# Three batches of q and k turned on TensorE from 128 partitions, and loads and weights in order of need

## The chip, the cores and the metric

The kernel runs on one core of a Trainium2 chip. The metric is the device time of one execution in microseconds (us); "the span" is the time from the first to the last instruction in a profiled execution, some 2 us less. Most fast executions of a kernel here agree within 1 to 1.5%. Each has a state, fast or slow, from its time against the fastest run of the same kernel; comparisons below use fast runs. A profile belongs to one execution.

Engines: PE is TensorE, DVE is VectorE, ACT is ScalarE, POOL is GpSimd, and SP is the engine whose queue issues nearly all DMAs here. "SPq" and "POOLq" are the queues. An "evacuation" is the copy of a matmul's or transpose's result out of PSUM, the memory that PE writes.

## The reference, cut to what matters

B = 8 batches, H = 8 heads, S = 576 tokens, 16 beacon keys and values ahead of them, D = 64. Then an FFN with three input weights and a maximum.

```python
scores = scale * q @ concat(beacon_k, k).T        # causal on the 576 tokens, beacons always seen
a = softmax(scores);  x = a @ concat(beacon_v, v) # x: 4608 tokens x 512
h = maximum(maximum(x @ w1, x @ w2), x @ w3)      # 512 -> 768
out = h @ w_out                                   # 768 -> 512, float32
```

## The kernel before

A "pair" is two heads of one batch; there are 32 pairs, numbered 0 to 31, four to a batch. Each pair needs q and k with D on the partitions, so q and k must be turned. Batches 0 and 1 are turned on PE; batches 2 to 7 are cast to bfloat16, stored to DRAM and fetched back by a transposing DMA into `qT` and `kT`. Attention of a pair and a share of the FFN alternate, so that PE has work while ACT computes exponentials.

Loads go through nine rotating staging buffers (`st`) and a list. Every cast of a staged item by `C(...)` issues the next load of the list:

```python
st_pool = tc.tile_pool(name="st", bufs=9)

def load_pair(p, k_queue=None):                     # 96 partitions, two runs of 1536 bytes in each
    ...
    queue.dma_start(
        out=st[0:QP, i * NQ2 : (i + 1) * NQ2].rearrange("p (h x) -> p h x", h=2),
        in_=src[b, hs].rearrange("h (p r) d -> p h (r d)", r=QR))      # QR = 6, QP = 96

loads = [L(load_pair, p, nc.scalar) for p in range(PPB)]
loads += [L(load_v, 0, 0), L(load_v, 0, 1)]
for b in range(1, B):
    loads += [L(load_pair, b * PPB + i) for i in range(PPB)]
    if b == 1:
        loads += [L(load_beacons, B_PE, B, bk32)]
    loads += [L(load_v, b, 0), L(load_v, b, 1)]

def C(fn, *a):
    def run():
        fn(*a)
        next_load()          # one load for one cast
    return run

def start():
    load_beacons(0, B_PE, bk32_0)
    next_load(10)
    ...                      # cast pair 0
    next_load()

# p is the first pair of batch b >= 2; plan entries are (pair, step)
at_step(p - 3, 0, L(open_dram, b))
at_step(p + 1, 0, C(cast_v, b, 0, by_pool))         # v is cast one pair after its batch has begun
at_step(p + 1, 1, C(cast_v, b, 1, by_pool))
for i in range(PPB):
    at_step(p + i - 4 + (p + i == 8), 0, C(cast_pair, p + i, by_pool, by_pool))
    at_step(p + i - 3, int(p + i == 8), L(store_pair, p + i))
    at_step(p + i - 2, 1, L(fetch_pair, p + i))
```

Loads, stores to DRAM, fetches and output stores stand in the one SP queue, in program order; only k of batch 0 goes by ACT's queue and the weights by POOL's. The masks of pairs 4 and later and all casts but pair 0's are POOL's.

The softmax here doesn't subtract the row's maximum and nothing guards it: scores larger than these inputs give would overflow.

Of the kernel before, what the change touches and what calls it, by code (L numbers as in the profile page):

```python
# [9 lines left out]
BF16 = mybir.dt.bfloat16  # L10
# [6 lines left out]
def kernel(  # L17
# [27 lines left out]

    QR = 6
    QP = S // QR
    HALF = S // 2
# [14 lines left out]
    B_PE = 2  # L63
# [88 lines left out]
    def load_pair(p, k_queue=None):  # L152
        b, g, j0 = place(p)
        hs = slice(head(g, j0), head(g, j0) + 2)
        st = new_stage(("pair", p))
        for i, (src, queue) in enumerate(((q, nc.sync), (k, k_queue or nc.sync))):
            queue.dma_start(  # L157
                out=st[0:QP, i * NQ2 : (i + 1) * NQ2].rearrange("p (h x) -> p h x", h=2),
                in_=src[b, hs].rearrange("h (p r) d -> p h (r d)", r=QR),
            )  # L160

    def cast_piece(p, i, cast, r0=0, r1=QR):
        st = stage["pair", p]
        if ("pair16", p, i) not in stage:
            stage["pair16", p, i] = pair_pool.tile([QP, QR, 2, D], BF16, name=f"p16{i}")
        cast(  # L166
            stage["pair16", p, i][:, r0:r1].rearrange("p r h d -> p h r d"),
            st[0:QP, i * NQ2 : (i + 1) * NQ2].rearrange(
                "p (h r d) -> p h r d", h=2, r=QR
            )[:, :, r0:r1],  # L170
        )
# [63 lines left out]
    def turn_beacons():  # L235
        ps = ffn_psum.tile([128, PPB, NB_PE], BF16, name="fps")
        for pi in range(PPB):
            nc.tensor.transpose(
                ps[:, pi],
                bk16_0[:, 2 * pi : 2 * pi + 2].rearrange("p h d -> p (h d)"),  # L240
                ident[0:NB_PE, 0:NB_PE],
            )
        by_act(bT, ps)
# [31 lines left out]
    def turn(p, i, ps):  # L275
        src = stage.pop(("pair16", p, i))
        for r in range(QR):
            nc.tensor.transpose(
                ps[:, r * QP : (r + 1) * QP],
                src[:, r].rearrange("p h d -> p (h d)"),  # L280
                ident[0:QP, 0:QP],
            )

    def evac_q(p, ps, copy):
        copy(
            qTs[p % NT].rearrange("d (p r) -> d p r", r=QR),
            ps.rearrange("d (r p) -> d p r", r=QR),
        )

    def evac_k(p, ps, copy):  # L290
        b, pi = divmod(p, PPB)
        kT = kTs[p % NT]
        copy(kT[:, 0:Nb], bT[:, pi, Nb * b : Nb * (b + 1)])
        copy(
            kT[:, Nb:NK].rearrange("d (p r) -> d p r", r=QR),
            ps.rearrange("d (r p) -> d p r", r=QR),
        )

    def turn_pair(p, apart, q_copy=None, k_copy=None):
# [3 lines left out]
        else:  # L303
            both = sc_psum.tile([128, 2, 1024], BF16, name="sc")
# [184 lines left out]
    for tb in range(n_tokb):  # L489
        last_b = (TOKB * (tb + 1) - 1) // S  # L490
        for ft in range(n_ft):
            for i in range(3):
                units.append((last_b, mm1_unit, (tb, ft, i)))
# [23 lines left out]
    loads = [L(load_pair, p, nc.scalar) for p in range(PPB)]  # L517
    loads += [L(load_v, 0, 0), L(load_v, 0, 1)]
    for b in range(1, B):
        loads += [L(load_pair, b * PPB + i) for i in range(PPB)]  # L520
        if b == 1:
            loads += [L(load_beacons, B_PE, B, bk32)]
        loads += [L(load_v, b, 0), L(load_v, b, 1)]
# [13 lines left out]
    def start():  # L537
        load_beacons(0, B_PE, bk32_0)
        keep_busy(12)
        next_load(10)  # L540
        by_pool(bk16_0, bk32_0)
        turn_beacons()
        cast_piece(0, 0, by_dve)
        cast_piece(0, 1, by_act, 0, 3)
        cast_piece(0, 1, by_dve, 3, QR)
        stage.pop(("pair", 0))
        next_load()
        turn_pair(0, True, q_copy=by_act)
# [15 lines left out]
    at_step(0, 3, L(load_w, 0, 0, FH))  # L564
    at_step(1, 0, C(cast_v, 0, 0, by_pool))
    at_step(1, 1, L(load_w, 1, 0, FH))
    at_step(1, 2, C(cast_v, 0, 1, by_pool))
    at_step(1, 3, L(load_w, 2, 0, FH))
    at_step(2, 2, C(cast_pair, 4, by_pool, by_pool))
    at_step(3, 0, L(load_w, 0, FH, d_ff))  # L570
    at_step(3, 1, L(load_w, 1, FH, d_ff))
    at_step(3, 2, C(cast_pair, 5, by_pool, by_pool))
    at_step(3, 3, L(load_w, 2, FH, d_ff))
    at_step(4, 0, L(load_w_out))
    at_step(4, 1, C(cast_pair, 6, by_pool, by_pool))
    at_step(4, 3, C(cast_v, 1, 0, by_pool))
    at_step(5, 0, C(cast_v, 1, 1, by_pool))
    at_step(5, 0, C(cast_pair, 7, by_pool, by_pool))
    at_pv(2, 0, 0, 0, 0, 1)
# [10 lines left out]
    at_step(4, 2, L(by_pool, bk16, bk32))  # L590
    for b in range(B_PE, B):
        p = b * PPB
        at_step(p - 3, 0, L(open_dram, b))
        at_step(p + 1, 0, C(cast_v, b, 0, by_pool))
        at_step(p + 1, 1, C(cast_v, b, 1, by_pool))
        for i in range(PPB):
            at_step(p + i - 4 + (p + i == 8), 0, C(cast_pair, p + i, by_pool, by_pool))
            at_step(p + i - 3, int(p + i == 8), L(store_pair, p + i))
            at_step(p + i - 2, 1, L(fetch_pair, p + i))

    def emit_all():
# [3 lines left out]
        for p in range(NPAIR):  # L605
# [3 lines left out]
            for s, gs in enumerate(steps(p)):  # L609
# [12 lines left out]
                else:  # L622
                    n_step += 1
                    allowed = (n_step - 1) * UPB / (2 * PPB) - 1
                emit_ffn(allowed)
                store_y(n_y)
# [6 lines left out]
                if not fine and nxt < B_PE * PPB and s == 0:  # L633
                    turn_pair(nxt, False, None, by_act)
# [50 lines left out]
```

## Time and profile before

340.59 us median of 3 runs (340.47 to 341.17). The profiled span was 338.9 us.

| stretch (bounds are the first scores of pairs 5 and 12) | us |
|---|---|
| start to pair 5 | 38.2 |
| pair 5 to pair 12 (seven pairs) | 79.8 |
| pair 12 to the end | 220.9 |

The windows view of the kernel before, one line for each stretch. Columns: the stretch and its length, busy time of PE, PE's weight loads, DVE, ACT and POOL with the number of instructions, the granted clock of TensorE, the mean busy share of the DMA engines, and GB/s.

```profile
0.00:38.20 38.20, 28.93 (x409) 15.59 (x410) 20.09 (x53) 21.13 (x31) 24.81 (x42) 1.00 1.12 222
38.20:118.00 79.80, 51.48 (x608) 25.11 (x616) 29.45 (x57) 29.77 (x46) 32.29 (x61) 0.85 1.04 219
118.00:338.90 220.90, 209.21 (x2329) 107.42 (x2352) 120.70 (x219) 89.46 (x136) 73.76 (x147) 0.98 0.60 137
```

In the middle stretch PE is busy 51.5 of 79.8 us, at a mean clock of 0.85, while the DMA engines are full at 219 GB/s. The waits view of PE in the same kernel names what it waits for (total us, times, longest):

```profile
PE sc L345 <- DMA kT<-k_dram: 17.3, 6, 9.5
PE pv L407 <- POOL at_sb L370: 12.5, 2, 6.3
```

The timeline of PE places them (start, duration, work, and in brackets the idle time before and what ended it): two waits for masks near 44 and 51 us, one for `kT` of pair 8 near 74 us.

```profile
50.51 0.42 PE L407 MATMUL pv<-at_sb,ones 128*32 128x288 bf16 x4 [6.21 <-POOL at_sb L370]
57.24 0.58 PE L407 MATMUL pv<-at_sb,ones 128*32 128x176 bf16 x6 [6.31 <-POOL at_sb L370]
...
83.94 0.90 PE L345 MATMUL sc<-qT,kT 64*128 64x288 bf16 x8 [9.49 <-DMA kT<-k_dram]
```

The first masks are late because POOL's queue stood at the cast of v of batch 1, which had not landed. The timeline of POOL from 48.66 us on:

```profile
48.66 1.46 POOL L210 CAST v_sb<-st 128x1536 bf16<-128x1536 f32 x1 [9.05 <-DMA st<-in_v_dram]
...
52.15 4.68 POOL L166 CAST p<-st 96x768 bf16<-96x768 f32 x6
56.78 1.73 POOL L370 TENSOR_SCALAR_AFFINE_SELECT at_sb<-at_sb 128x256 bf16<-128x256 bf16 x5
```

```profile
143.38 0.54 PE L345 MATMUL sc<-qT,kT 64*128 64x288 bf16 x8 [2.03 <-DMA kT<-k_dram]
...
175.92 0.56 PE L345 MATMUL sc<-qT,kT 64*128 64x288 bf16 x8 [2.04 <-DMA kT<-k_dram]
...
209.96 0.54 PE L345 MATMUL sc<-qT,kT 64*128 64x288 bf16 x8 [1.94 <-DMA kT<-k_dram]
```

### The profile page before, as it was taken

What the parts mean: (1) busy time and instruction counts of PE and PEld (TensorE: products, weight loads), DVE (VectorE), ACT (ScalarE), POOL (GpSimd) and SP (SyncE); (2) the same over time, 40 slices, a digit from 0 to 9 for tenths busy, and PEclk for the clock granted to TensorE, in tenths of its full rate; (3) what the DMA queues carried; (4) which work ended last, traced back from release to release, by engine and by line L of the source; (5) the groups of instructions that cost most, each with busy time, mean ns of one, the idle gap of its engine ahead of it and who ended that gap; (6) DMA issues with size and microseconds to landing.
All of it is one profiled execution on the core that took longest, in us unless ns stands there. A gap on an engine that the chain in (4) does not pass through costs nothing.

```text
span 338.9 us, 8218 instructions
## 1 busy us (share of the span) xinstructions
PE 289.6 (85%) x3342; PEld 148.1 (44%) x3372; DVE 170.2 (50%) x328; ACT 140.4 (41%) x212; POOL 130.9 (39%) x249
## 2 busy tenths in 40 slices
PE   4798622870998999799979997999999999999995
PEld 2345301330443454354435455774445445444442
DVE  0686400650546454545554555455675666555453
ACT  2468730340444564365434643454554642020220
POOL 1795529212364346345623562356523320000000
PEclk9999975995899999999998999899999999999999
DMA  8999999999959996999899979945740400301203
GB/s 198 218 248 240 196 219 242 214 241 228 227 149 239 222 242 182 230 227 200 243 222 207 162 235 217 169 112 161 141 72 35 130 0 4 124 0 49 78 0 124
DMA packets 97814, 56.32 MB, mean 166 GB/s; under 512 B 72432, under 2 KB 93168, under 8 KB 97776
## 3 DMA queue, kind: packets, MB, share of 16 engines
q1 hardware_dynamic: 92896, 51.47, 68.3%
q0 software_dynamic: 4048, 3.15, 6.0%
q10 hardware_dynamic: 832, 1.18, 1.4%
q8 instruction: 26, 0.43, 0.5%
q14 instruction: 12, 0.10, 0.1%
HBM read 35.13 MB, written 16.61 MB: 153 GB/s over the span
## 4 chain that ended last, share of the span: by engine, by line
PE 68%; DMA 8%; SPq 3%; issue 2%; DVE 1%; POOL 1%; DVEq 0%
PE fps L453 33%; PE fps L470 11%; PE pv L407 10%; PE sc L345 7%; DMA kT<-k_dram 5%; PE sc L453 5%; DMA st<-in_q_dram 2%; PE sc L470 2%; SPq L194 1%; SPq L270 1%; SPq L263 1%; SPq L157 1%; POOL at_sb L370 0%; DVE hT L463 0%; DVE xT L430 0%
## 5 line engine op out<-in xcount | busy, mean ns | idle before, releaser
L354 ACT ACTIVATE at_sb<-sc 128x992 bf16<-128x992 f32 (+3 forms) x128 | 103.9, 861 | 115.7 <-PE sc L345 115.5
L453 PE MATMUL fps<-xT,w_sb 128*128 128x512 bf16 (+1 forms) x623 | 137.5, 357 | 1.7 <-issue 0.7
L463 DVE TENSOR_TENSOR hT<-hT,fps 128x512 bf16<-128x512 bf16 x95 | 65.2, 686 | 74.4 <-PE fps L453 72.2
L453 PEld LDWEIGHTS <-w_sb 128*128 128x128 bf16 x720 | 67.1, 98 | 73.0 <-issue 14.3
L370 POOL TENSOR_SCALAR_AFFINE_SELECT at_sb<-at_sb 128x256 bf16<-128x256 bf16 (+2 forms) x140 | 51.0, 384 | 116.8 <-ACT at_sb L354 116.8
L345 PE MATMUL sc<-qT,kT 64*128 64x288 bf16 (+4 forms) x384 | 38.5, 297 | 21.2 <-DMA kT<-k_dram 17.3
L166 POOL CAST p<-st 96x768 bf16<-96x768 f32 x62 | 49.3, 824 | 18.2 <-DMA q_dram<-p 9.8
L461 DVE CAST hT<-fps 128x512 bf16<-128x512 f32 x42 | 28.9, 687 | 27.3 <-PE fps L453 27.3
L470 PE MATMUL fps<-w_out_sb,hT 128*128 128x512 bf16 x173 | 41.7, 380 | 0.8 <-DVE hT L463 0.4
L478 DVE COPY y<-fps 128x512 f32<-128x512 f32 x30 | 20.7, 689 | 30.3 <-PE fps L470 30.3
L345 PEld LDWEIGHTS <-kT 64*128 64x128 bf16 x384 | 14.0, 96 | 48.9 <-issue 25.2
L407 PE MATMUL pv<-at_sb,v_sb 128*32 128x96 bf16 (+8 forms) x1408 | 32.3, 243 | 0.0
L407 PE MATMUL pv<-at_sb,ones 128*32 128x288 bf16 (+4 forms) x512 | 19.6, 272 | 14.4 <-POOL at_sb L370 12.5
L430 DVE TENSOR_TENSOR xT<-pv,recip 128x288 bf16<-128x288 f32 (+2 forms) x96 | 28.1, 348 | 6.4 <-ACT recip L427 3.8
L470 PEld LDWEIGHTS <-hT 128*128 128x128 bf16 x216 | 20.0, 98 | 25.8 <-issue 2.0
L407 PEld LDWEIGHTS <-v_sb 128*32 128x32 bf16 (+1 forms) x1408 | 26.6, 103 | 2.8 <-issue 0.8
L210 POOL CAST v_sb<-st 128x1536 bf16<-128x1536 f32 (+2 forms) x24 | 21.0, 894 | 9.4 <-DMA st<-in_v_dram 9.4
L425 ACT ACTIVATE lnd<-pv 128x288 f32<-128x288 f32 x32 | 13.2, 412 | 24.0 <-PE pv L407 23.3
L407 PEld LDWEIGHTS <-ones 128*32 128x32 bf16 (+1 forms) x512 | 11.4, 100 | 22.3 <-issue 17.8
L453 PE MATMUL sc<-xT,w_sb 128*128 128x512 bf16 x74 | 19.2, 379 | 0.1
L427 ACT ACTIVATE recip<-lnd 128x288 f32<-128x288 f32 x32 | 14.2, 443 | 1.0
L461 ACT CAST hT<-fps 128x512 bf16<-128x512 f32 x6 | 3.5, 586 | 22.7 <-PE fps L453 22.7
(38 smaller groups left out, 90.1 us busy)
## 6 DMA issues: line engine op xcount, KB each, us to landing
st<-in_q_dram SPq DMA_DIRECT2D x32, 288.0 KB, 4.4
out_dram<-y SPq DMA_DIRECT2D x36, 256.0 KB, 2.3
st<-in_k_dram SPq DMA_DIRECT2D x28, 288.0 KB, 4.7
st<-in_v_dram SPq DMA_DIRECT2D x24, 256.0 KB, 5.5
q_dram<-p SPq DMA_DIRECT2D x24, 144.0 KB, 2.7
k_dram<-p SPq DMA_DIRECT2D x24, 144.0 KB, 2.8
w_sb<-in_moe_w_dram POOLq DMA_DIRECT2D x12, 192.0 KB, 11.3
st<-in_v_dram SPq DMA_DIRECT2D x8, 224.0 KB, 5.6
```

Source lines behind the costliest of these rows:

```text
L166: cast(stage["pair16", p, i][:, r0:r1].rearrange("p r h d -> p h r d"), st[0:QP, i * NQ2 : (i + 1) * NQ2].rearrange("p (h r d) -> p h r d" ...
L210: cast(v_sb[0:n, t:t1].rearrange("p t h d -> p (t h d)"), st[0:n, (t - t_lo) * H * D : (t1 - t_lo) * H * D],)
L345: nc.tensor.matmul(ps[:, e, off : off + q1 - q0], kT[hs, 128 * t : 128 * t + 128], qT[hs, q0:q1], start=True, stop=True, tile_position=(64 ...
L354: nc.scalar.activation(out=both_heads(p, gi), in_=ps[:, :, 0 : g_width[gi]], func=AF.Exp, scale=scale)
L370: nc.gpsimd.affine_select(out=view, in_=view, compare_op=ALU.is_ge, fill=0.0, base=x0, pattern=[[0, 2], [1, hi - lo]], channel_multiplier=-1,)
L407: nc.tensor.matmul(ps[32 * j : 32 * j + 32, bank, lo + q0 - qa : lo + qb - qa], lhsT, at_view(PPQ * quad + j // 2, t, j % 2, q0, qb), star ...
L430: nc.vector.tensor_mul(xT[:, 2 * g + part - 1, c0 + ca : c0 + cb], ps[:, bank, lo : lo + cb - ca], recip[:, ca:cb],)
L453: nc.tensor.matmul(ps[:, o0 : o0 + n], w_in[i][:, ct, 128 * ft : 128 * (ft + 1)], xT[:, ct, x0 : x0 + n], start=(ct == 0), stop=(ct == n_c ...
L461: (by_act if alone[0] else by_dve)(hT[:, ft, :], ps)
L463: nc.vector.tensor_max(hT[:, ft, :], hT[:, ft, :], ps)
L470: nc.tensor.matmul(ps, hT[:, ft, 128 * tt : 128 * (tt + 1)], w_out_sb[:, ft, :], start=(ft == 0), stop=(ft == n_ft - 1),)
L478: nc.vector.tensor_copy(y, ps)
```

## The change

Intent: (1) q and k of batches 0 to 2 land on all 128 partitions (each head on 64, nine rows of 256 bytes in a run) and are turned by 64 by 64 transposes, two side by side; so batch 2 no longer goes through DRAM, and its pairs are cast two pairs ahead of their use, not four. (2) The FFN takes one weight after the other within a block, so that w2, w3 and w_out may come later, and the weights are loaded whole, half of them behind v of batch 1. (3) Pair 0's loads come first; the second group of beacon loads comes later; the FFN's pace is a little faster at the start.

```diff
-    B_PE = 2
+    B_PE = 3
@@ load_pair
+            if b < B_PE:
+                queue.dma_start(
+                    out=st[:, i * PR * D : (i + 1) * PR * D],                       # PR = 9
+                    in_=src[b, hs].rearrange("h (p r) d -> (h p) (r d)", r=PR))
@@ turn
-        for r in range(QR):
-            nc.tensor.transpose(ps[:, r * QP : (r + 1) * QP], src[:, r]..., ident[0:QP, 0:QP])
+        for r in range(PR):
+            for e in range(2):
+                hs = slice(64 * e, 64 * e + 64)
+                nc.tensor.transpose(ps[hs, r * PP : (r + 1) * PP], src[hs, r],
+                                    ident[hs, hs], tile_position=(64 * e, 64 * e))
@@ FFN units
-        for ft in range(n_ft):
-            for i in range(3):
+        for i in range(3):
+            for ft in range(n_ft):
@@ list of loads
+    loads = [L(load_pair, 0, nc.scalar), L(load_beacons, 0, B_PE, bk32_0)]
+    loads += [L(load_pair, 1, nc.scalar)] + load_pairs(2, 4) + load_v_pieces(0)
+    loads += load_pairs(4, 8) + load_v_pieces(1)
+    loads += load_pairs(8, 12) + load_v_pieces(2) + [L(load_beacons, B_PE, B, bk32)]
+    for b in range(B_PE, B): ...
@@ start
-        load_beacons(0, B_PE, bk32_0)
         next_load(10)
@@ weights
-    (w1, w2, w3 in halves at pairs 0, 1 and 3, w_out at pair 4)
+    at_step(1, 1, L(load_w, 0, 0, d_ff))
+    at_step(3, 1, L(load_w, 1, 0, d_ff))
+    at_step(4, 2, L(load_w, 2, 0, d_ff))
+    at_step(5, 1, L(load_w_out))
@@ casts of batch 2
+    for p in range(8, B_PE * PPB):
+        at_step(p - 2, 1, C(cast_pair, p, by_pool, by_pool))
@@ emit_all
-                    allowed = (n_step - 1) * UPB / (2 * PPB) - 1
+                    allowed = n_step * UPB / 9 if n_step <= 9 else (n_step - 1) * UPB / (2 * PPB)
@@ (cut: the turn moves from the first to the second step of a pair and into another PSUM pool;
@@  evacuations, the other casts and the order of the start follow; k of pairs 2 and 3 now comes by SP)
```

More of the change, by code (lines that the diff above doesn't have):

```diff
@@ L47 @@
     QP = S // QR
+    PR = 9
+    PP = S // PR
     HALF = S // 2
@@ L156, in load_pair, with cast_piece @@
         for i, (src, queue) in enumerate(((q, nc.sync), (k, k_queue or nc.sync))):
-            queue.dma_start(
-                out=st[0:QP, i * NQ2 : (i + 1) * NQ2].rearrange("p (h x) -> p h x", h=2),
-                in_=src[b, hs].rearrange("h (p r) d -> p h (r d)", r=QR),
-            )
-    def cast_piece(p, i, cast, r0=0, r1=QR):
-        st = stage["pair", p]
-        if ("pair16", p, i) not in stage:
-            stage["pair16", p, i] = pair_pool.tile([QP, QR, 2, D], BF16, name=f"p16{i}")
-        cast(
-            stage["pair16", p, i][:, r0:r1].rearrange("p r h d -> p h r d"),
-            st[0:QP, i * NQ2 : (i + 1) * NQ2].rearrange(
-                "p (h r d) -> p h r d", h=2, r=QR
-            )[:, :, r0:r1],
-        )
+            if b < B_PE:
+                queue.dma_start(
+                    out=st[:, i * PR * D : (i + 1) * PR * D],
+                    in_=src[b, hs].rearrange("h (p r) d -> (h p) (r d)", r=PR),
+                )
+            else:
+                queue.dma_start(
+                    out=st[0:QP, i * NQ2 : (i + 1) * NQ2].rearrange("p (h x) -> p h x", h=2),
+                    in_=src[b, hs].rearrange("h (p r) d -> p h (r d)", r=QR),
+                )
+    def cast_piece(p, i, cast):
+        st = stage["pair", p]
+        if p < B_PE * PPB:
+            t16 = pair_pool.tile([128, PR, D], BF16, name=f"t16{i}")
+            cast(
+                t16.rearrange("x r d -> x (r d)"), st[:, i * PR * D : (i + 1) * PR * D]
+            )
+        else:
+            t16 = pair_pool.tile([QP, QR, 2, D], BF16, name=f"p16{i}")
+            cast(
+                t16.rearrange("p r h d -> p h r d"),
+                st[0:QP, i * NQ2 : (i + 1) * NQ2].rearrange("p (h r d) -> p h r d", h=2, r=QR),
+            )
+        stage["pair16", p, i] = t16
     def cast_pair(p, q_cast, k_cast):
@@ L235, in turn_beacons @@
     def turn_beacons():
-        ps = ffn_psum.tile([128, PPB, NB_PE], BF16, name="fps")
+        ps = pv_psum.tile([128, PPB, NB_PE], BF16, name="pv")
         for pi in range(PPB):
@@ L276, in turn @@
         src = stage.pop(("pair16", p, i))
-        for r in range(QR):
-            nc.tensor.transpose(
-                ps[:, r * QP : (r + 1) * QP],
-                src[:, r].rearrange("p h d -> p (h d)"),
-                ident[0:QP, 0:QP],
-            )
+        for r in range(PR):
+            for e in range(2):
+                hs = slice(64 * e, 64 * e + 64)
+                nc.tensor.transpose(
+                    ps[hs, r * PP : (r + 1) * PP],
+                    src[hs, r],
+                    ident[hs, hs],
+                    tile_position=(64 * e, 64 * e),
+                )
     def evac_q(p, ps, copy):
         copy(
-            qTs[p % NT].rearrange("d (p r) -> d p r", r=QR),
-            ps.rearrange("d (r p) -> d p r", r=QR),
+            qTs[p % NT].rearrange("d (p r) -> d p r", r=PR),
+            ps.rearrange("d (r p) -> d p r", r=PR),
         )
@@ L294, in evac_k @@
         copy(
-            kT[:, Nb:NK].rearrange("d (p r) -> d p r", r=QR),
-            ps.rearrange("d (r p) -> d p r", r=QR),
+            kT[:, Nb:NK].rearrange("d (p r) -> d p r", r=PR),
+            ps.rearrange("d (r p) -> d p r", r=PR),
         )
@@ L303, in turn_pair @@
         else:
-            both = sc_psum.tile([128, 2, 1024], BF16, name="sc")
+            both = pv_psum.tile([128, 2, 1024], BF16, name="pv")
             q_ps, k_ps = both[:, 0, 0:S], both[:, 1, 0:S]
@@ L515, in L, with load_v_pieces, load_pairs @@
         return lambda: fn(*a)
-    loads = [L(load_pair, p, nc.scalar) for p in range(PPB)]
-    loads += [L(load_v, 0, 0), L(load_v, 0, 1)]
-    for b in range(1, B):
-        loads += [L(load_pair, b * PPB + i) for i in range(PPB)]
-        if b == 1:
-            loads += [L(load_beacons, B_PE, B, bk32)]
-        loads += [L(load_v, b, 0), L(load_v, b, 1)]
+    def load_v_pieces(b):
+        return [L(load_v, b, 0), L(load_v, b, 1)]
+    def load_pairs(p0, p1):
+        return [L(load_pair, p) for p in range(p0, p1)]
+    loads = [L(load_pair, 0, nc.scalar), L(load_beacons, 0, B_PE, bk32_0)]
+    loads += [L(load_pair, 1, nc.scalar)] + load_pairs(2, 4) + load_v_pieces(0)
+    loads += load_pairs(4, 8) + load_v_pieces(1)
+    loads += load_pairs(8, 12) + load_v_pieces(2) + [L(load_beacons, B_PE, B, bk32)]
+    for b in range(B_PE, B):
+        loads += load_pairs(b * PPB, (b + 1) * PPB) + load_v_pieces(b)
     def next_load(n=1):
@@ L537, in start @@
     def start():
-        load_beacons(0, B_PE, bk32_0)
-        keep_busy(12)
+        keep_busy(14)
         next_load(10)
+        cast_piece(0, 0, by_dve)
+        cast_piece(0, 1, by_act)
+        stage.pop(("pair", 0))
         by_pool(bk16_0, bk32_0)
-        turn_beacons()
-        cast_piece(0, 0, by_dve)
-        cast_piece(0, 1, by_act, 0, 3)
-        cast_piece(0, 1, by_dve, 3, QR)
-        stage.pop(("pair", 0))
-        next_load()
-        turn_pair(0, True, q_copy=by_act)
+        next_load()
+        q_ps = ffn_psum.tile([128, S], BF16, name="fps")
+        k_ps = ffn_psum.tile([128, S], BF16, name="fps")
+        turn(0, 0, q_ps)
+        turn(0, 1, k_ps)
+        evac_q(0, q_ps, by_act)
+        turn_beacons()
+        evac_k(0, k_ps, by_dve)
         C(cast_pair, 1, by_pool, by_pool)()
@@ L563 @@
     at_step(0, 2, C(cast_pair, 3, by_pool, by_pool))
-    at_step(0, 3, L(load_w, 0, 0, FH))
     at_step(1, 0, C(cast_v, 0, 0, by_pool))
-    at_step(1, 1, L(load_w, 1, 0, FH))
+    at_step(1, 1, L(load_w, 0, 0, d_ff))
     at_step(1, 2, C(cast_v, 0, 1, by_pool))
-    at_step(1, 3, L(load_w, 2, 0, FH))
-    at_step(2, 2, C(cast_pair, 4, by_pool, by_pool))
-    at_step(3, 0, L(load_w, 0, FH, d_ff))
-    at_step(3, 1, L(load_w, 1, FH, d_ff))
-    at_step(3, 2, C(cast_pair, 5, by_pool, by_pool))
-    at_step(3, 3, L(load_w, 2, FH, d_ff))
-    at_step(4, 0, L(load_w_out))
-    at_step(4, 1, C(cast_pair, 6, by_pool, by_pool))
-    at_step(4, 3, C(cast_v, 1, 0, by_pool))
+    at_step(1, 3, C(cast_pair, 4, by_pool, by_pool))
+    at_step(2, 3, C(cast_pair, 5, by_pool, by_pool))
+    at_step(3, 1, L(load_w, 1, 0, d_ff))
+    at_step(4, 0, C(cast_pair, 6, by_pool, by_pool))
+    at_step(4, 1, C(cast_v, 1, 0, by_pool))
+    at_step(4, 2, L(load_w, 2, 0, d_ff))
     at_step(5, 0, C(cast_v, 1, 1, by_pool))
     at_step(5, 0, C(cast_pair, 7, by_pool, by_pool))
+    at_step(5, 1, L(load_w_out))
+    for p in range(8, B_PE * PPB):
+        at_step(p - 2, 1, C(cast_pair, p, by_pool, by_pool))
+    for b in range(2, B):
+        p = b * PPB
+        at_step(p + 1, 0, C(cast_v, b, 0, by_pool))
+        at_step(p + 1, 1, C(cast_v, b, 1, by_pool))
     at_pv(2, 0, 0, 0, 0, 1)
@@ L589 @@
         at_pv(2 * quad + 3, 0, quad, 1)
-    at_step(4, 2, L(by_pool, bk16, bk32))
+    at_step(7, 1, L(by_pool, bk16, bk32))
     for b in range(B_PE, B):
@@ L593 @@
         at_step(p - 3, 0, L(open_dram, b))
-        at_step(p + 1, 0, C(cast_v, b, 0, by_pool))
-        at_step(p + 1, 1, C(cast_v, b, 1, by_pool))
         for i in range(PPB):
-            at_step(p + i - 4 + (p + i == 8), 0, C(cast_pair, p + i, by_pool, by_pool))
-            at_step(p + i - 3, int(p + i == 8), L(store_pair, p + i))
+            at_step(p + i - 4, 0, C(cast_pair, p + i, by_pool, by_pool))
+            at_step(p + i - 3, 0, L(store_pair, p + i))
             at_step(p + i - 2, 1, L(fetch_pair, p + i))
@@ L623, in emit_all @@
                     n_step += 1
-                    allowed = (n_step - 1) * UPB / (2 * PPB) - 1
+                    allowed = n_step * UPB / 9 if n_step <= 9 else (n_step - 1) * UPB / (2 * PPB)
                 emit_ffn(allowed)
+                if not fine and nxt < B_PE * PPB and s == 1:
+                    turn_pair(nxt, False)
                 store_y(n_y)
@@ L632, in emit_all @@
                 finish_pv()
-                if not fine and nxt < B_PE * PPB and s == 0:
-                    turn_pair(nxt, False, None, by_act)
                 while emit_ffn(allowed):
```

## The prediction

> **What bounds the kernel now.** The windows view splits the 338.9 us into three regimes. From 118 us on TensorE is nearly always busy (most 20 us windows: 18 to 19.9 us); the change alters little there. From 0 to 38 us pairs 0 to 4 run at about 5 us each, set by the exponentials and the chain between PE, ACT and DVE. From 38 to 93 us TensorE starves at a DMA share near 1.1: the waits view gives PE 12.5 us on the masks (near 44 and 51 us) and 9.5 us on kT of pair 8 (at 74 us), at a granted clock of 0.5 to 0.87. The timeline shows why. First, GpSimd sits 9.05 us for v of batch 1 (cast at 48.7 us), because four weights (3.15 MB) and six beacon loads shared the engines ahead of it. Second, pair 8's store leaves the SP queue only at 75.7 us, behind saturated loads, and then needs a transposing fetch.
>
> **Removed.** Ahead of v of batch 1, the data fall from about 10.5 MB (the slices' GB/s summed to 48.6 us) to about 8.7 MB; at the measured 220 GB/s that is 8 to 9 us, so v lands near 40 us and the first stall shrinks from 12.5 to about 3 us. Batch 2 loses its DRAM round trip: 16 transfers of 144 KB, 2.3 MB, about 10 us of DMA, with the 9.5 us wait and kT waits of 1.6 and 0.2 us near 110 and 118 us. Pair 0 comes first: the first scores (11.4 us) gain 2 us.
>
> **Added.** A pair's turn goes from 12 transposes (0.68 us warm, 1.14 cold) to 36. The Trainium skill's "TensorEngine Tiling (Array Packing)", section Instruction Overhead, gives about 60 cycles per matmul, hence my estimate of 0.9 to 1.2 us warm, 1.5 to 2 us cold: about 8 us over twelve pairs, 3 of them hidden. DVE gets 8 more evacuations of 0.75 us, off the path. FFN weight by weight only lets w2, w3 and w_out come late.
>
> **On the path.** PE's work between pair 5's and pair 12's first scores: seven pairs of attention (2.5 us each), six turns (1.1), 35 FFN units (148 matmuls at 0.228 us): 58 us, against 79.8 us now (38.2 to 118.0). With 3 us for v and 2 to 4 us where GpSimd meets pair 12's load too early (14.7 MB must have moved, 66 us), pair 12 starts at 102 to 105 us instead of 118. That is 15 us, of which 0 to 2 are given back later through longer kT waits. Tail unchanged.
>
> **Predicted:** 325 us, 8 in 10 between 315 and 334. Faster by over 2%: 0.86; within 2%: 0.11; slower: 0.03.
>
> **What shows it.** The timeline: pair 12's first scores near 103 us; v of batch 1 cast near 40 us; no DMA wait at pair 8; PE waits on masks under 5 us; 36 transposes in 0.9 to 1.2 us; from pair 12 to the end still 220 to 223 us.
>
> **What would make it wrong.** GpSimd's in-order queue: a cast waiting for a late load (v of batch 1 now stands before pair 4's last masks; pair 12's cast) blocks masks, so stalls move instead of vanish. Late w3 or w_out would stall the FFN. The DMA, still behind at pair 12, could make kT waits recur. The 64 by 64 transposes may not overlap in pairs, and cost 2 us or more warm.

## The result, and the profile after

308.34 us median of 4 runs (306.05 to 309.71), against 340.88 us (340.47 to 345.34) for the kernel before over the runs by then. The ratio is 0.9012, 95% interval 0.8919 to 0.9105: faster. A ratio is the mean time of one kernel's fast runs over that of the other's of the same rounds, so it is not quite the ratio of the medians. The profile is of the fastest run, with a span of 304.3 us. The measured time lies below the predicted range of 315 to 334 us.

The windows view of the kernel after, cut at the first scores of pairs 5 and 12 as before:

```profile
0.00:37.00 37.00, 29.44 (x556) 16.52 (x556) 20.08 (x52) 21.44 (x31) 17.62 (x34) 1.00 1.04 260
37.00:93.20 56.20, 51.42 (x798) 26.03 (x812) 36.99 (x73) 28.28 (x42) 30.77 (x63) 1.00 1.03 242
93.20:304.30 211.10, 204.52 (x2325) 105.14 (x2348) 120.24 (x218) 89.45 (x136) 73.89 (x148) 1.00 0.64 146
```

| stretch | before, us | after, us | predicted, us |
|---|---|---|---|
| start to pair 5 | 38.2 | 37.0 | about 38 |
| pair 5 to pair 12 | 79.8 | 56.2 | 64 to 67 (pair 12 at 102 to 105) |
| pair 12 to the end | 220.9 | 211.1 | 220 to 223 |

So 23.6 us were gained where the prediction expected about 15, and 9.8 us where it expected nothing. In the middle stretch PE is busy as long as before (51.4 us), but of 28.3 us of idle time 4.8 are left, and the clock stays at 1.00. The waits of PE on masks and on `kT` by DMA are gone from the profile; in their place stand small waits on DVE's evacuation of the turn:

```profile
PE sc L361 <- DVE kT L310: 5.6, 6, 2.8
PE pv L423 <- DVE xT L446: 1.5, 3, 0.6
```

The timeline of PE shows a turn of 36 transposes in 0.76 us, and pair 15, which waited 2.03 us before, starting without a gap:

```profile
41.50 0.76 PE L293 MATMUL pv<-ident,t 64*64 64x64 bf16 x36
...
113.69 2.84 PE L469 MATMUL fps<-xT,w_sb 128*128 128x512 bf16 x12
116.47 0.54 PE L361 MATMUL sc<-qT,kT 64*128 64x288 bf16 x8
```

And POOL casts v of batch 1 with no wait, at 34.7 and 39.9 us (48.66 and 51.04 before), in the timeline of POOL:

```profile
34.74 1.46 POOL L223 CAST v_sb<-st 128x1536 bf16<-128x1536 f32 x1
...
39.86 1.16 POOL L223 CAST v_sb<-st 128x512 bf16<-128x512 f32 x2
```

Of the 9.8 us after pair 12, the three `kT` waits at pairs 15, 19 and 23 in the kernel before (its timeline of PE is above) are 6.0 us (2.03 + 2.04 + 1.94). Another 3.2 us are a low clock: from pair 19 to 20 and from 23 to 24 the kernel before took 8.7 us, where it took 7.1 from pair 15 to 16 with the same work. In the windows view of the kernel before, around pair 19, the clock falls after the gap:

```profile
171.00:173.00 2.00, 2.00 (x11) 0.90 (x10) 1.55 (x5) 1.56 (x2) 0.77 (x2) 1.00 1.02 195
173.00:175.00 2.00, 0.88 (x4) 0.19 (x2) 1.36 (x2) 0.00 (x0) 0.04 (x1) 1.00 1.11 149
175.00:177.00 2.00, 1.08 (x20) 0.74 (x24) 0.00 (x0) 0.59 (x1) 0.00 (x0) 0.83 0.87 292
177.00:179.00 2.00, 2.00 (x60) 1.67 (x56) 0.00 (x0) 1.08 (x2) 1.53 (x4) 0.50 1.00 247
```

The question is then what removed these waits, since nothing in the change is addressed to pairs 15, 19 and 23, and what fed the middle stretch faster than foreseen.

### The profile page after: what moved, and what is told of

It is laid out like the page before. It is cut to its first block, busy times and chain, and to the rows that moved or that the text cites. A ratio compares the mean times of both kernels' runs of the same rounds, so it can differ in the third digit from the quotient of the medians.

```text
span 304.3 us, 8877 instructions
## 1 busy us (share of the span) xinstructions
PE 285.4 (94%) x3673; PEld 147.7 (49%) x3710; DVE 177.3 (58%) x343; ACT 139.2 (46%) x208; POOL 122.3 (40%) x243
## 4 chain that ended last, share of the span: by engine, by line
PE 86%; DVE 6%; issue 2%; ACT 2%; DMA 1%; SPq 0%; POOL 0%; POOLq 0%; DVEq 0%
PE fps L469 41%; PE pv L423 12%; PE fps L486 12%; PE sc L361 10%; PE sc L469 5%; PE sc L486 2%; DVE qT L301 1%; DVE kT L310 1%; DMA bk<-in_beacon_k_dram 1%; PE fps L330 1%; DVE xT L446 1%; DVE hT L479 1%; ACT at_sb L370 1%; DVE kT L309 1%; PE fps L293 1%
## 5 line engine op out<-in xcount | busy, mean ns | idle before, releaser
L469 PEld LDWEIGHTS <-w_sb 128*128 128x128 bf16 x720 | 65.7, 97 | 71.0 <-issue 13.4
L386 POOL TENSOR_SCALAR_AFFINE_SELECT at_sb<-at_sb 128x256 bf16<-128x256 bf16 (+2 forms) x140 | 51.1, 384 | 114.5 <-ACT at_sb L370 114.5
L361 PE MATMUL sc<-qT,kT 64*128 64x288 bf16 (+4 forms) x384 | 37.7, 294 | 6.3 <-DVE kT L310 5.6
L486 PE MATMUL fps<-w_out_sb,hT 128*128 128x512 bf16 x172 | 40.6, 379 | 1.0 <-issue 0.8
L180 POOL CAST p<-st 96x768 bf16<-96x768 f32 x40 | 31.8, 822 | 0.0
L423 PE MATMUL pv<-at_sb,v_sb 128*32 128x96 bf16 (+8 forms) x1408 | 29.4, 230 | 0.0
L423 PEld LDWEIGHTS <-v_sb 128*32 128x32 bf16 (+1 forms) x1408 | 24.4, 97 | 2.2 <-issue 0.9
L423 PE MATMUL pv<-at_sb,ones 128*32 128x288 bf16 (+4 forms) x512 | 17.5, 258 | 1.6 <-DVE xT L446 1.5
L469 PE MATMUL sc<-xT,w_sb 128*128 128x512 bf16 x71 | 18.3, 380 | 0.1
L479 DVE TENSOR_TENSOR hT<-hT,sc 128x512 bf16<-128x512 bf16 x12 | 8.2, 687 | 12.5 <-PE sc L469 6.8
```

The costliest lines, as they stand in the source:

```text
L180: cast(t16.rearrange("p r h d -> p h r d"), st[0:QP, i * NQ2 : (i + 1) * NQ2].rearrange("p (h r d) -> p h r d", h=2, r=QR),)
L361: nc.tensor.matmul(ps[:, e, off : off + q1 - q0], kT[hs, 128 * t : 128 * t + 128], qT[hs, q0:q1], start=True, stop=True, tile_position=(64 ...
L386: nc.gpsimd.affine_select(out=view, in_=view, compare_op=ALU.is_ge, fill=0.0, base=x0, pattern=[[0, 2], [1, hi - lo]], channel_multiplier=-1,)
L423: nc.tensor.matmul(ps[32 * j : 32 * j + 32, bank, lo + q0 - qa : lo + qb - qa], lhsT, at_view(PPQ * quad + j // 2, t, j % 2, q0, qb), star ...
L469: nc.tensor.matmul(ps[:, o0 : o0 + n], w_in[i][:, ct, 128 * ft : 128 * (ft + 1)], xT[:, ct, x0 : x0 + n], start=(ct == 0), stop=(ct == n_c ...
L479: nc.vector.tensor_max(hT[:, ft, :], hT[:, ft, :], ps)
```

## The experiments

Eighteen kernels ran, all with correct results. "Pair 12 at" is the start of its first scores in the profile of that kernel. Kernels of one call share the runs of the kernel before, whose median was 340 to 344 us in each call; so a difference between calls is better read from the ratios, which use fast runs alone. The medians count all runs: without its one slow run, a_lead has 322.6, b_wide 332.5 and less_again 306.4 us. The profile of b_wide is of its slow run.

| kernel | edit, on the kernel before (b) or after (a) | median, us | ratio to before | pair 12 at |
|---|---|---|---|---|
| before | | 340.6 | 1 | 118.0 |
| after | | 308.3 | 0.901 | 93.2 |
| b_lead, b_less | nine, eight loads at the start, not ten | 327.4, 323.1 | 0.959, 0.947 | 113.1, 110.2 |
| a_lead | one load more ahead | 323.2 | 0.943 | 95.5 |
| b_wide | wide loads, batches 0 and 1 | 333.6 | 0.974 | 114.5 |
| b_order | weights and FFN in order of need | 340.4 | 0.997 | 119.4 |
| b_wol, b_wol_less | all three; nine, eight loads | 323.1, 320.1 | 0.945, 0.931 | 110.3, 107.0 |
| a_desc | wide loads in runs of 768 bytes | 313.1 | 0.916 | 99.3 |
| a_ft | FFN units in the old order | 314.8 | 0.922 | 102.5 |
| a_wearly | weights early and in halves | 314.7 | 0.918 | 101.8 |
| a_pace | the old pace of the FFN | 309.7 | 0.908 | 95.8 |
| after_again | none | 307.9 | 0.903 | 95.5 |
| a_lead_less, less_again | eight loads at the start | 305.7, 306.8 | 0.893, 0.899 | 92.3, (disturbed) |
| best3, best_lead, best_bpe4 | attempts at a faster kernel | 309.9, 305.7, 311.0 | 0.907, 0.893, 0.907 | 95.6, 92.5, 93.4 |
| a_probe | five layouts of loads behind the end | | | |

### The lead of the loads

The lead is how many loads have been issued ahead of the casts that use them. Each cast issues one load. The list of the kernel after has two beacon items, that of the kernel before had one, and a beacon item uses up a cast's turn without using a staging buffer. From there on every load of the kernel after is issued one cast later than before. Why that can matter: a load needs the buffer of the item nine places earlier in the list, but v of a batch is cast later than its place in the list (at the second pair of its batch, when the first pair of the next batch is already cast). With the longer lead the newest load must wait for that cast; it waits at the head of SP's queue, and the stores and fetches behind it wait too. The Trainium skill says in "DMA: Bandwidth & Descriptors", section "Anatomy of one DMA — SWDGE (gpsimd) path", that a semaphore wait of a DMA is done on the issuing sequencer before dispatch. The timeline of SP in the kernel before agrees: after the fetch at 124.23 us the queue issues nothing for 3.7 us, then the load that had waited for v's buffer and all that had gathered behind it, and the fetch for pair 15, due at 141.4, leaves at 138.8 and 140.7 us.

```profile
124.23 1.27 SPq L271 DMA_TRANSPOSE kT<-k_dram  x1
129.24 0.31 SPq L157 DMA_DIRECT2D st<-in_q_dram  x1
...
138.77 1.86 SPq L270 DMA_TRANSPOSE qT<-q_dram  x1
140.67 1.26 SPq L271 DMA_TRANSPOSE kT<-k_dram  x1
```

In the waits view of SP, the loads' wait for v's buffer is, in the kernel before from pair 12 to pair 31 and in the kernel after over the whole span:

```profile
SPq L157 <- POOL v_sb L210: 11.0, 3, 3.7
SPq L166 <- POOL v_sb L223: 1.6, 1, 1.6
```

In the kernel after, the same fetch leaves at 110.0 and 111.2 us, for a pair that starts at 116.5. The rival was that there is simply less DMA traffic, since batch 2 no longer goes through DRAM.

**a_lead** gives the kernel after the old lead back.

```diff
-    loads += load_pairs(8, 12) + load_v_pieces(2) + [L(load_beacons, B_PE, B, bk32)]
+    loads += load_pairs(8, 12) + load_v_pieces(2)
+    at_step(4, 1, L(load_beacons, B_PE, B, bk32))
```

> The kernel after, but the second beacon load is issued on its own instead of taking one turn in the list of loads, so every later load is issued one cast earlier (the lead the kernel before had). Theory (SP's in-order queue is held by a load that waits for a staging buffer, and the fetches behind it come late): SP waits on the casts of v return (16 us in total before, 1.6 us after), PE waits about 2 us for kT at pairs 15, 19 and 23 again, and the time rises by 5 to 9 us over 308. Rival (the waits vanished because there is less DMA traffic): no kT waits, within 2 us of 308.

323.22 us median (321.77 to 326.86, one of them slow), 15 us over the kernel after, more than expected. In the waits view of PE stands:

```profile
PE sc L361 <- DMA kT<-k_dram: 12.7, 4, 3.9
```

The waits view of SP in the same kernel, from 93 us to 256 us, has the wait for v's buffers again:

```profile
SPq L166 <- POOL v_sb L223: 12.3, 3, 4.1
```

The waits stand at pairs 12, 15, 19 and 23 (2.64, 3.12, 3.93, 2.97 us), and the clock is 0.50 to 0.60 after the first three and 1.00 after the fourth. From pair 12 to pair 31 it took 160.6 us, against 145.2 in the kernel after and 154.5 in the kernel before. Why these waits are longer than the three of 2 us in the kernel before was not traced.

**b_lead** takes one item of lead from the kernel before, **b_less** two; nothing else.

```diff
-        next_load(10)
+        next_load(9)       # b_lead;  next_load(8) in b_less
```

> The kernel before, with nine loads issued at the start instead of ten, so every load comes one cast later; nothing else. Theory (lead): the three 2 us kT waits at pairs 15, 19 and 23 shrink or vanish, with the low clock that follows two of them, and the time falls by 5 to 9 us from 341 to about 333. Rival (DMA traffic of batch 2's round trip): the waits stay, 339 to 342.

> The kernel before with eight loads at the start instead of ten (b_lead had nine: 327.4 us). If the order in SP's queue still costs there, the kT wait of pair 8 (9.5 us before, 7.3 us with nine) falls to 3 to 6 us and the time to 321 to 326. If pair 8 waits for bytes, not for order: 326 to 330.

b_lead: 327.43 us median (326.44 to 328.88), 13 us or more gained by one number, where 5 to 9 were expected. From pair 12 to pair 31 it took 145.2 us, exactly as in the kernel after, though batch 2 still went through DRAM: the lead alone accounts for the whole gain between those pairs, and the rival falls. Pair 12 itself comes 4.9 us earlier. SP's waits view from 113 to 258 us:

```profile
SPq L157 <- POOL v_sb L210: 3.3, 3, 1.7
```

b_less: 323.07 us (320.38 to 325.11). Its wait for pair 8 fell to 3.4 us as expected, and it has the mask waits that the kernel before had, as the waits view of PE in b_less shows:

```profile
PE pv L407 <- POOL at_sb L370: 12.4, 2, 6.3
PE sc L345 <- DMA kT<-k_dram: 3.7, 2, 3.4
```

Pair 8 starts at 77.9 us, 6 us earlier than before. So a part of the early stall at pair 8 was the place of its store and fetch behind loads that were not needed yet. b_order and b_wol below show what is left.

### The rate of the loads

**b_wide** puts only the wide layout (and its transposes) for batches 0 and 1 into the kernel before. The diff is the `load_pair` and `turn` parts shown above with `B_PE = 2`.

> The kernel before, with only the layout of q and k of batches 0 and 1 changed to 128 partitions and 36 small transposes; batch 2 still goes through DRAM, weights and order as before. Theory (DMA rate): v of batch 1 is cast about 5 to 6 us earlier than 48.7 us, the two mask waits (12.5 us) shrink to about 7, kT of pair 8 is still waited for, and the time falls by 4 to 9 us from 341. Rival (only the order of the weights matters): 339 to 344.

333.59 us median of 4, one of them slow; the fast ones 331.27 to 334.67, ratio 0.974 (0.964 to 0.985), which does not settle "over 2%" by its interval. The profile fell in the slow run. A gain of about 9 us is at the upper end of what was expected, although the transposes tripled in number. In that profile v of batch 1 was cast at 44.4 us, 4.3 us earlier and not 5 to 6, and the mask waits were 10.7 us, not about 7: 6.3 of them are still the casts of pairs 7 to 9.

**a_desc** keeps the 128 partitions but lands each run of 2304 bytes as three of 768.

```diff
-                    out=st[:, i * PR * D : (i + 1) * PR * D],
-                    in_=src[b, hs].rearrange("h (p r) d -> (h p) (r d)", r=PR),
+                    out=gapped(st, i),        # three pieces of 192 floats in each 256
+                    in_=src[b, hs].rearrange("h (p c r) d -> (h p) c (r d)", c=3, r=3),
```

> The kernel after, with each partition's 2304 contiguous bytes of a pair load of batches 0 to 2 landed as three runs of 768 bytes with gaps, same partitions, same bytes, same order. Theory (longer runs move faster: 350 to 390 GB/s against 250 to 275): the GB/s while pairs load fall to 250 or lower, v of batch 1 lands later by 5 us or more, PE waits for masks or kT before pair 12 come back, and the time rises by 4 to 12 us over 308. Rival (order and number of bytes alone made the difference): within 2 us of 308.

313.13 us (311.12 to 314.33), 5 us slower, with 3.23 us of wait at pair 12 (which says little: the unchanged kernel has 3.27 us there in its second profile, below). The DMA view of its first microseconds shows some 260 to 360 GB/s while pairs load, not 250: the theory of run length failed on the number it was built on. But the short runs did slow the start: the first 40 us moved 224 GB/s, against 267 and 250 in the two profiles of the kernel after, and pair 5 came at 39.8 us, against 37.0 and 35.6.

**a_probe** therefore measures layouts by themselves, behind the end of the kernel after: blocks of four loads of 288 KB, each block waiting for the one before, five layouts, twice.

```diff
+        def wide(b, n, hs):         # 128 partitions, 2304 bytes
+            nc.sync.dma_start(out=probe[n][:, 0:576], in_=q[b, hs].rearrange("h (p r) d -> (h p) (r d)", r=9))
+        def wide_short(b, n, hs):   # 128 partitions, 768 bytes
+            ...
+        def narrow(b, n, hs):       # 96 partitions, 1536 bytes: the layout before
+            ...
+        def narrow_long(b, n, hs):  # 96 partitions, 3072 bytes
+            nc.sync.dma_start(out=probe[n][0:96, 0:768], in_=q[b, hs].rearrange("h (p r) d -> (h p) (r d)", r=12))
+        def half(b, n, hs):         # 64 partitions, 2304 bytes
+            ...
```

> The kernel after with ten blocks of four loads of 288 KB behind its end (some 45 us longer, so its total time says nothing), each block waiting for the one before: five layouts, each twice. Theory of partitions (the Trainium skill, SBUF - State Buffer, section Door 1: partitions 0 to 63 and 64 to 127 are reached by different halves of 16 ports, so 96 partitions load one half twice as much as the other, an estimate of 3/4 of the full rate): 128 partitions with 2304 or 768 byte runs 300 to 380 GB/s, 96 partitions with 1536 or 3072 byte runs both 230 to 290, 64 partitions 170 to 220. Theory of run length: 96 partitions with 3072 bytes and 64 with 2304 as fast as 128 with 2304; 128 with 768 the slowest.

Its 384 us, of one run of unknown state, include the ten blocks. The windows view, one stretch in the middle of the first block of each layout, in the order of the list above; the columns are as before, the last two are the DMA share and GB/s:

```profile
309.50:311.00 1.50, 0.00 (x0) 0.00 (x0) 0.00 (x0) 0.00 (x0) 0.00 (x0) 0.54 1.02 366
316.50:318.00 1.50, 0.00 (x0) 0.00 (x0) 0.00 (x0) 0.00 (x0) 0.00 (x0) 0.50 1.13 349
324.50:326.50 2.00, 0.00 (x0) 0.00 (x0) 0.00 (x0) 0.00 (x0) 0.00 (x0) 0.50 1.08 245
331.50:333.50 2.00, 0.00 (x0) 0.00 (x0) 0.00 (x0) 0.00 (x0) 0.00 (x0) 0.50 1.03 272
339.00:341.50 2.50, 0.00 (x0) 0.00 (x0) 0.00 (x0) 0.00 (x0) 0.00 (x0) 0.50 1.05 207
```

In the middle of a block the number of partitions decides most: 366 and 349 GB/s on 128, 245 and 272 on 96, 207 on 64; the second blocks give 375, 316, 254, 260 and 208 in stretches of the same length. The length of the runs counts too, and more over a whole block. From the first issue to the landing of all four loads, by the timelines of SP and DVE, it took 6.3 and 6.0 us for 128 partitions with long runs, 7.1 and 7.0 with short ones, 6.8 and 6.7 for the layout before, 6.4 and 6.6 for 96 partitions with long runs, 8.1 and 8.4 for 64. So short runs took from 128 partitions all that they gain over the layout before, which fits the 5 us of a_desc, and for a group of four loads the wide layout saves a tenth, not a third. The DMA share is about 1 in every line, so a full share is not a full rate. The Trainium skill, "SBUF — State Buffer", section Door 1, gives a reason: partitions 0 to 63 reach one half of 16 ports, 64 to 127 the other half, so 96 partitions put two thirds of the bytes on one half. That this is the mechanism is the page's word; the runs show the rates. In the kernels themselves the DMA moved 8.85 MB in the first 40 us before and 10.67 MB after (10.0 MB in the second profile of the kernel after; 9.7 MB in b_wide).

### The order of weights and of the FFN

**b_order** moves only the weights, and the FFN order they need, in the kernel before (the two diffs above).

> The kernel before, with only the weights moved to their places in the kernel after (whole w1, w2, w3 and w_out, half of them behind v of batch 1) and the FFN weight by weight; narrow loads, DRAM for batch 2 and the lead as before. Theory (bytes ahead of v): v of batch 1 is cast 6 to 9 us earlier than 48.7 us, mask waits fall from 12.5 to 3 to 7 us, but kT of pair 8 is waited for all the longer because the same bytes must still move, so only 3 to 8 us of 341 are gained. Rival (order of need alone carries most of the gain): 15 us or more.

340.44 us against 340.18 in the same rounds, ratio 0.997 (0.990 to 1.004): the same, below what was expected. It did shorten the mask waits from 12.5 to 6.1 us (POOL waited 2.6 us for v, not 9.05; the casts of pairs 7 to 9 stayed ahead of the masks), and the wait for pair 8 grew from 9.5 to 15.7 us, so that pair 8 starts at 85.1 us against 83.9. A stall taken away ahead of a later deadline returns at that deadline.

**a_wearly** brings the weights back to their early places in the kernel after.

> The kernel after, with all the weights loaded as early and in the halves of the kernel before; all else as after. Theory (bytes ahead of v of batch 1, at a rate of about 250 GB/s): 1.6 MB more go first, so v lands 5 to 7 us later than its cast is due at 34.7 and 39.9 us, masks wait, pairs 6 and on start 4 to 7 us later, and since the same bytes must have moved by pair 12 a part of it is won back there: 310 to 315 us. Rival (wide loads alone are fast enough): within 2 us of 308.

314.65 us (313.65 to 315.85), 6 us over the kernel after. POOL waits 10.16 us for v of batch 1 (cast at 44.5 us), PE 6.1 us for masks, and nothing is won back at pair 12, which comes at 101.8 us. So the order of the weights is worth nothing alone and 6 us where pair 8 no longer waits for DRAM.

**a_ft** takes only the FFN order back.

> The kernel after, with the FFN units of a block in their old order (all three weights for one slice of d_ff before the next), weights still loaded whole and in order of need. Theory: w3 is issued at 36.5 us and lands 8 to 9 us later, but would now be needed at its third unit, near 40 us: PE waits 3 to 8 us for w3 at pair 5 or 6, and again for w_out not at all; time 311 to 317. Rival (the order of units does nothing): within 2 us of 308.

314.75 us (314.51 to 315.34), with the wait where it was expected; this is the timeline of PE:

```profile
45.75 0.60 PE L469 MATMUL fps<-xT,w_sb 128*128 128x512 bf16 x2 [3.61 <-DMA w_sb<-in_moe_w_dram]
48.79 1.04 PE L469 MATMUL fps<-xT,w_sb 128*128 128x512 bf16 x2 [2.44 <-DMA w_sb<-in_moe_w_dram]
```

The new FFN order is what allows the late weights; what it costs by itself was not measured.

**a_pace** restores the old formula for `allowed`.

> The kernel after with the FFN units let go at the old pace (one unit later throughout, over three units later during pairs 5 to 8). PE has less to do before pair 12 and more later: pair 12 comes earlier than 93 us and then waits for kT (DMA bound, near 93 to 95 us), the units left over go to the tail: 308 to 313 us. If the pace does nothing, within 1 us of after_again.

309.67 us (308.55 to 310.35) against 307.92 for after_again in the same rounds. Pair 12 came later, not earlier (95.8 us), and had no `kT` wait, so that part of the expectation was wrong. The difference of under 2 us was not traced.

### What turning batch 2 on PE gives

**b_wol** and **b_wol_less** have wide loads, order of need and a shorter lead; batch 2 still goes through DRAM.

> The kernel before with the wide layout for batches 0 and 1, the order of weights and the FFN order of the kernel after, and one load less of lead: all but turning batch 2 on PE, the pace and the start. If the three parts explain the result, pair 12's first scores come at 96 to 104 us, a kT wait of 2 to 8 us remains at pair 8, no kT waits recur from pair 12 on, and the time is 311 to 320 us; what is left over the kernel after is what batch 2 on PE adds. If turning batch 2 on PE is what matters most, 322 us or more.

> The kernel before with wide loads for batches 0 and 1, order of need, and eight loads at the start (b_wol had nine: 323.1 us, with 11.3 us of wait for kT at pair 8). If SP's order makes that wait, it falls to 3 to 7 us as it did from b_lead (7.3) to b_less (3.4), and the time to 314 to 319; what then is left above 306 (the kernel after with the same lead) is what turning batch 2 on PE gives. If pair 8 waits for bytes: 321 to 324.

323.11 us (321.86 to 323.72) and 320.14 us (318.62 to 320.57). The wait for `kT` of pair 8 stays at 11.3 and 8.3 us, and pair 8 starts at 77.5 and 74.0 us, hardly earlier than in b_less. b_wol met the alternative that batch 2 on PE matters most (322 us or more); b_wol_less fell between its two. The waits view of PE in b_wol_less:

```profile
PE sc L360 <- DMA kT<-k_dram: 8.3, 1, 8.3
PE pv L422 <- POOL at_sb L385: 4.4, 1, 4.4
```

The kernel after with the same `next_load(8)`, a_lead_less below, takes 305.7 us, 13 to 15 us less. By the two profiles 13.8 us of this lie between pairs 5 and 12 (70.0 against 56.3 us), and 12.7 of them are those two waits. The first is the round trip through DRAM. The second is POOL casting pairs 7, 8 and 9 ahead of the masks, as in the kernel before: v had landed, but pairs that go through DRAM are cast early, for their store and fetch. So most of the 13 to 15 us comes with batch 2 on PE; the new start and pace are in the difference too and were not separated here. Neither the order nor the lead that was tried let the round trip meet its deadline at pair 8.

### A faster kernel

**a_lead_less** and **less_again** are the kernel after with `next_load(8)` for `next_load(10)`; **after_again** is the kernel after, unchanged, in the rounds of less_again.

> The kernel after, with eight items loaded at the start instead of ten, so every load comes two casts later and stands less far ahead of the stores and fetches in SP's queue. Theory (the lead is what delays the fetches): no kT waits by DMA in any pair, SP's waits on the casts of v near 0, the early part the same as long as the DMA still has work queued, 305 to 309 us with less spread than after (306 to 310). Rival (less lead starves the DMA): waits of GpSimd on loads of v and pairs appear before pair 12, over 311 us.

> The kernel after, unchanged, to stand in the same rounds as less_again. 306 to 310 us; if its spread comes from the fetch of pair 12 arriving just in time or just too late, a profile above 307 us shows a kT wait of 1 to 4 us at pair 12 and a low clock behind it.

> The kernel after with eight items loaded at the start instead of ten (a_lead_less again), same rounds as after_again. If the lead is what leaves the kernel after at the edge: 305 to 307 us, 1.5 to 3.5 us less than after_again. If the earlier difference was between chips and calls only: equal within 1 us.

a_lead_less: 305.65 us (305.15 to 306.77). after_again: 306.31 to 310.50, and its profile, of the slowest run, shows the wait at pair 12 that the first profile of this kernel did not have; the clock was then 0.52 to 0.63 for 4 us:

```profile
95.55 0.54 PE L362 MATMUL sc<-qT,kT 64*128 64x288 bf16 x8 [3.27 <-DMA kT<-k_dram]
```

From pair 5 to pair 12 it took 60.0 us, not 56.2. So the kernel after sits at the edge of a deadline at pair 12, the first pair that still goes through DRAM. less_again's five fast runs took 305.83 to 307.24 us; their mean is 306.5 against 308.2 for the six of after_again, a ratio of 0.995 worked out from these times. It is steadier and slightly faster, well under 2%. One execution of less_again, the profiled one, took 968.79 us and counts as slow: its FFN matmuls with the three input weights lasted 996 ns in the mean, against 355 in the kernel after, with a recorded clock of 1.0. No run explains it, and it is used for nothing.

**best3** puts the turn one FFN unit earlier and lets ACT copy the first beacon columns; **best_lead** is best3 with `next_load(8)`; **best_bpe4** is best3 with batch 3 on PE too.

```diff
+                if not fine and nxt < B_PE * PPB and s == 1:
+                    turn_pair(nxt, False)
                 emit_ffn(allowed)
-                if not fine and nxt < B_PE * PPB and s == 1:
-                    turn_pair(nxt, False)
@@ start
+        by_act(kTs[0][:, 0:Nb], bT[:, 0, 0:Nb])
```

> An attempt at a faster kernel on top of the kernel after. The turn of the next pair is put one FFN unit earlier in the second half of a pair, so that its evacuations end before the next scores: the five waits of 0.2 to 0.7 us of PE on kT by DVE (2.9 us at pairs 6 to 10) vanish. At the start the beacon columns of kT are copied by ACT, not by DVE, where that copy took 1.69 us beside GpSimd's casts: first scores 1.5 to 2 us earlier than 10.1 us. Together 2 to 5 us: 303 to 306 us. If the first pairs are bound otherwise, only 2 us.

> The attempt best3 (earlier turn, ACT for the first beacon columns) with eight items loaded at the start instead of ten. best3 had gained 2.3 us by pair 11 (83.7 against 86.0 us) and lost 4.75 us waiting for kT of pair 12. Two loads (1.2 MB, about 5 us) now stand behind that fetch instead of ahead of it: the wait falls to under 1 us, and the time to 303 to 306 us. If it only moves, 308 to 311.

> best3 with batch 3 turned on PE as well (five batches fewer or more through DRAM: four left). PE pays four turns of 0.76 us, the DMA loses another 2.4 MB and the first fetch is due at pair 16 instead of 12: no kT wait at pair 12, 303 to 307 us. If the DMA is not what bounds pair 12, 311 or more.

best3: 309.91 us, no gain, where 303 to 306 were expected. It reached pair 11 at 83.7 us, 2.3 us ahead of the kernel after, and then waited 4.75 us for pair 12, the deadline again. best_lead: 305.65 us (305.35 to 307.08); the wait is gone, but it is not faster than a_lead_less. best_bpe4: 311.02 us, with four batches left through DRAM, and again not the gain expected. There is no wait at pair 12, but pairs 12 to 16 took 34.1 us where the kernel after takes 30.4: PE is the bound there, and each of the three turns in this stretch costs it 1.2 us, 0.76 us of transposes and the rest waits around them. With PE free of waits, moving more work to it is a loss. The best kernel found is the kernel after with eight loads at the start, some 10% under the kernel before.

## Why the prediction was wrong

- **Direction and place: right.** The two stalls it named, masks behind v of batch 1 and `kT` of pair 8, both vanished in the first profile, and the middle stretch gave most of the gain. v of batch 1 was cast at 34.7 and 39.9 us, near the predicted 40.
- **PE's work between pairs 5 and 12: near, but too high.** It predicted 58 us; PE was busy for 51.4 of the 56.2 us, and 2.9 us of the rest are waits on DVE. Six turns took 0.76 us each, not 1.1, which makes up 2 us.
- **Failed: "3 us for v and 2 to 4 us where GpSimd meets pair 12's load too early", on "the measured 220 GB/s".** The term was mis-sized: both waits were zero in the first profile. First, the rate. Up to pair 12 the kernel after moved 249 GB/s in the mean. By the windows of 10 us, 8.7 MB had moved by some 33 us, not 40, and 14.7 MB by 60 us, not 66. So v was there when its cast was due, and pair 12's load at its cast at 62.8 us. The wide layout raises the rate (b_wide, a_probe), and one rate had been used for both layouts; but no run puts the old layout into the kernel after, so its share there is argued. Second, the stall. Only 6.2 of the 12.5 us of mask waits were v's; the other 6.3 were POOL casting pairs 7 to 9 ahead of the masks, and the change casts pairs 8 and 9 later. In the second profile POOL waited 2.2 us for v without costing PE a mask wait, and PE waited 3.3 us at pair 12: that this wait was zero in the first profile was partly luck.
- **Failed: "of which 0 to 2 are given back later", "from pair 12 to the end still 220 to 223 us".** The sign was wrong: 9.8 us were won there, 6.0 us of waits and 3.2 us of clock. The cause is one item less of lead, a side effect of a second beacon entry in the list of loads. a_lead brought the waits back, b_lead removed them with nothing else changed. The three waits of 2 us were in the profile before; the prediction took them for DMA traffic and did not ask SP's waits what held the fetches.
- **Related, in the same step: the cause of the stall at pair 8.** It was put to a store "behind saturated loads". b_less shows that two items of lead bring pair 8 from 83.9 to 77.9 us; b_order shows that late weights alone only move the wait; b_wol_less shows that 8.3 us stay with both.
- **The risks it listed:** one occurred in part, the `kT` wait at pair 12 (3.3 us in the second profile). No late weight stalled the FFN in the kernel after (6 us once the FFN order was undone), and 36 transposes took 0.76 us, not 2 or more.

The parts do not add up to the whole: by the ratios, in the kernel before a lead shorter by one and by two items gave 14 and 18 us, wide loads 9, order 1 (the same, by its interval); all three with eight loads at the start 24; and batch 2 on PE, with the new start and pace, 13 more.

## What to carry to other kernels

A queue that issues in order turns prefetching too far ahead into a delay of what is needed next: when short waits recur with a period, look at what holds the head of the issuing queue, and try a smaller lead before anything larger. Cost a DMA by its layout, the partitions it reaches and the length of its runs, not by the mean rate of the old kernel. When an engine comes late with something, look whether it waited or worked: half of the mask waits here were POOL's own casts, put too early. Taking away one stall pays only up to the next deadline, and an engine that has lost its waits has no room for more work.

## What the Trainium skill lacked or had wrong

- "SBUF — State Buffer", section Door 1, has rates for 64 and 128 partitions (196 and 328 GB/s at 1 MiB) but none for 96. Here 64, 96 and 128 partitions reached 207 to 208, 245 to 272 and 316 to 375 GB/s with four loads of 288 KB in flight. The page's direction is right.
- "TensorE: Matmul & The Clock Gate", section Why this matters for your kernels, advises against idle gaps over about 3 us. Here gaps of 2.04 and 1.94 us were followed by a clock of 0.50, at pairs 19 and 23 of the kernel before, and one of 2.03 us at pair 15 was not; in a_lead gaps of 2.64, 3.12 and 3.93 us were followed by 0.50 to 0.60 and one of 2.97 us was not. So the length of the one gap did not decide it.
- "TensorEngine Tiling (Array Packing)", section Instruction Overhead, gives about 60 cycles for a matmul, from which 0.9 us was estimated for 36 transposes of 64 columns. Warm, they took 0.76 us, two tiles side by side.
- "DMA: Bandwidth & Descriptors" says that the issuing sequencer waits before dispatch, but not what that costs other DMAs behind it: in the kernel before 11.0 us of SP's queue after pair 12 went into waiting for buffers of v, and 6.0 us of PE into the fetches behind.
- No page has an execution like that of 968.79 us, with FFN matmuls of 996 ns over the whole span at a recorded clock of 1.0; a caveat that records of the clock can be wrong is the nearest.
